# A fused SSM and two-MLP kernel on one Trainium2 core: token sums and rounding remainders of the next block pair moved to other places in the order, more tiles of their own for pair 1, and another order at the end

## The chip, the cores and the metric

One NeuronCore of a Trainium2 chip runs the whole program. The metric is the device time of one execution in microseconds (us). Five engines matter: TensorE (PE, matmuls into PSUM), VectorE (DVE), ScalarE (ACT), GpSimd (POOL) and SyncE (SP, which issues most transfers). Each runs its own list of instructions in order.

## The reference

The inputs are a small state-space layer and two MLPs on its output, all in float32. The second MLP is the part that the change touches.

```python
attn_out = _attn_ref(**attn_kwargs)            # 3072 tokens, 256 features
x = np.ascontiguousarray(attn_out.transpose(0, 2, 1, 3)).reshape(B * S, H * D)
h = x @ w_in                                   # 256 -> 2048
g = np.where(h > 0.0, h, np.exp(np.minimum(h, 0.0)) - 1.0)
x = g @ w_out                                  # 2048 -> 256
g = x @ w_gate                                 # 256 -> 1536
silu = g * (1.0 / (1.0 + np.exp(-g)))
val = x @ w_val                                # 256 -> 1536
out = silu * val @ w_out                       # 1536 -> 256, the second MLP's own w_out
```

(`w_gate`, `w_val` and the last `w_out` belong to the second MLP.)

## The kernel before, in words

Features lie on the 128 partitions and tokens along the free axis. The 3072 tokens are six blocks of 512. The state-space layer and the first MLP run block by block (16 steps of 128 hidden features each, 96 steps in all); the second MLP then takes the blocks in three pairs, p = 0, 1, 2, with 12 steps of 128 hidden features for a pair, 36 steps j = 0 to 35 (`s_step`, L729). The whole order is written out by hand: inside a step it is the order of the calls, and further work is hung on a step by `at(...)`. For the first MLP the table `late` holds work that follows a step; for the second MLP the table `hooks` holds it at four places of a step, `a` (before L770), `b` (before L777), `c` (before L784) and `d` (at the end), and `o` before the output products.

**Two parts for each operand.** A float32 value is split into a rounded part `h` (an ACT copy to the type float32r) and the remainder `l` = value minus `h` (a subtraction). A product then takes three matmuls, `h` x `h`, `l` x `h` and `h` x `l`. `x_hi` (L691) and `x_lo` (L706) do this for the tokens, `w2_hi` (L662) and `w2_lo` (L668) for the weights, `g_split` (L747) for the gated hidden values.

**Seven products for two blocks.** The gate and value products of a pair of blocks are formed with seven 128x512 products in place of eight. This needs sums of token tiles, `t3` = b22 - b12, `t1` = b12 - b11, `t2` = b22 - t1, `t4` = b21 - t2 (`x_sum`, L684; the b are quarters of the pair's tokens), and sums of weight tiles (`w2_sums`, L653, on POOL). The seven token operands of a step are, in order of use, b11, t2, t3, t1, b21, t4, b22.

**A step.** PE issues 33 matmuls: three each for b11 into PSUM tile `pa`, t2 into `pb`, t3 into `pd`, t1 into `pc`, then b21 onto `pa`, t4 onto `pd`, b22 onto `pc`, then twelve output products of the step before (`s_o`, L713, with the tiles `gh` and `gl`). The second product may be added onto `pd` only after DVE has read the first one. Beside it run, for each step:

```python
ACT  s1 = pa (L758);  s5 = pc (L764);  m0 = silu(pa) (L775);  m1 = silu(u2) (L781);  gh (L749), twice
DVE  u2 = s1 + pb (L762);  u3 = u2 + pd (L763);  u3 += s5 (L770);  s1 = u2 + pd (L777)
DVE  u2 = u2 + pc (L778);  m0 *= s1 (L779);  m1 *= u3 (L784)
POOL gl = m - gh (L750), twice
```

In steps 1 to 9 DVE has besides the remainder of a weight tile in two pieces (L670, at `b` and at `d`), ACT the rounding of it (L666), and POOL the four weight sums (L655 to L658), whose tile a transfer brings in (L651).

**The next pair.** For p = 1, 2 with e = 12p the sums of the pair's tokens stand on POOL at `c` of steps e-5 to e-2. The rounding (ACT, L704) and the remainders (DVE, t4's on POOL, L708) stand in steps e-3 to e-1; the remainders at `d`, b22's at `a` of step e. Operands b11, t2 and t3 of pair 1 have tiles of their own (b11 and t2 in the two staging tiles `v2` of the weights once these are done, t3 in a tile of the pool `w2h`); all others of pair 1 and all of pair 2 reuse pair 0's tiles.

**The end of a pair.** `s_end` (L720) copies the four PSUM outputs of a pair to SBUF, two on DVE (L724) and two on ACT (L726), and SP sends each to HBM (L727): for pairs 0 and 1 in the second step of the next pair, for pair 2 after the last step. Half of the copies go to two tiles `yo`, the other half into a finished token block.

## Time and profile before

| | us |
|---|---|
| median of three runs | 621.52 |
| the three runs | 621.55, 617.13, 621.52 |
| the profiled execution | 621.05 |
| its span, first to last instruction | 619.3 |
| mean granted clock of TensorE, share of full | 0.999 |

The profiled execution's time contains its span and what lies around it (1.75 us). The rows below are from this one execution. The times are from the start of the span; "idle before" is idle time of the engine directly before the instruction, with what ended it. A matmul's row lasts 0.39 us, but matmuls overlap: they begin 0.23 us apart, so the distance of starts tells PE's pace. The second MLP runs from 329.4 us to the end.

### The profile page before, as it was taken

To read this page: it belongs to the slowest core of one execution; us is meant where nothing else is said; L and a number is where in the kernel's file an instruction comes from. 1 tells how busy PE (TensorE), PEld (TensorE's weight loads), DVE (VectorE), ACT (ScalarE), POOL (GpSimd) and SP (SyncE) were. 2 spreads that over 40 slices of the span, in tenths; PEclk is the share of its full clock that TensorE was granted. 3 is DMA by queue.
4 is the path that set the end of the run, shared out by engine and by line. 5 is a ranking of instruction groups with operands and counts; after the bars stand their busy time and mean duration, and the time that the engine had idled before them with its cause. 6 is when DMAs were issued, how large, how long until landed. Compare 5 with 4: busy or idle time off the path is not lost.

```text
span 619.3 us, 9832 instructions
## 1 busy us (share of the span) xinstructions
PE 596.2 (96%) x3524; PEld 469.7 (76%) x3524; DVE 468.5 (76%) x676; ACT 369.6 (60%) x659; POOL 365.0 (59%) x326
## 2 busy tenths in 40 slices
PE   6899999999999999999999999978999998999997
PEld 4556667888888888778878777866888886888885
DVE  6898866768878789795644999899666679766664
ACT  1456657776668667776876555545544455544443
POOL 4444559997887887774765666756333456333332
PEclk9999999999999999999999999999999999999999
DMA  7698533345466666622010011100100000100001
GB/s 210 214 287 244 180 100 113 111 138 174 164 178 207 203 200 205 212 78 78 25 52 23 29 52 52 52 1 0 69 1 1 1 0 1 69 1 1 1 0 68
DMA packets 22744, 58.70 MB, mean 95 GB/s; under 512 B 3736, under 2 KB 6168, under 8 KB 22696
## 3 DMA queue, kind: packets, MB, share of 16 engines
q1 hardware_dynamic: 20664, 53.18, 27.6%
q10 hardware_dynamic: 2032, 4.90, 2.1%
q8 instruction: 27, 0.44, 0.3%
q14 instruction: 21, 0.17, 0.1%
HBM read 50.12 MB, written 7.96 MB: 94 GB/s over the span
## 4 chain that ended last, share of the span: by engine, by line
PE 62%; issue 10%; DVE 6%; POOL 5%; DMA 4%; ACT 1%; POOLq 0%; DVEq 0%; ACTq 0%
PE h L556 16%; PE c L605 15%; PE o L556 10%; PE pd L742 5%; POOL gl L750 5%; PE pa L742 5%; PE pc L742 4%; DMA w2e<-in_w 4%; PE pb L742 3%; PE cb L432 1%; PE y L509 1%; PE c L597 1%; DVE w2l L670 1%; DVE ident L763 1%; DVE ident L762 1%
## 5 line engine op out<-in xcount | busy, mean ns | idle before, releaser
L750 POOL TENSOR_TENSOR gl<-m,gh 128x512 fp32r<-128x512 f32 x71 | 94.6, 1333 | 133.6 <-ACT gh L749 133.6
L562 POOL TENSOR_TENSOR gl<-m,gh 128x512 fp32r<-128x512 f32 x80 | 110.6, 1383 | 43.5 <-ACT gh L561 42.1
L584 DVE SCALAR_TENSOR_TENSOR m<-m,h 128x512 f32<-128x512 f32 x96 | 65.5, 683 | 55.1 <-ACT m L583 53.2
L578 ACT ACTIVATE m<-h 128x512 f32<-128x512 f32 x96 | 56.8, 592 | 48.4 <-PE h L556 42.4
L556 PE MATMUL h<-xh,wih 128*128 128x512 f32 x192 | 81.3, 424 | 2.9 <-DVE x L477 1.9
L556 PE MATMUL h<-xh,wil 128*128 128x512 f32 x192 | 76.1, 396 | 0.0
L605 PE MATMUL c<-gh,woh 128*128 128x512 f32 x160 | 62.4, 390 | 0.0
L605 PE MATMUL c<-gh,wol 128*128 128x512 f32 x160 | 62.3, 389 | 0.0
L583 ACT ACTIVATE m<-m 128x512 f32<-128x512 f32 x96 | 59.8, 623 | 0.5
L556 PE MATMUL h<-xl,wih 128*128 128x512 f32 x192 | 59.8, 393 | 0.0
L781 ACT ACTIVATE m<-ident 128x512 f32<-128x512 f32 x36 | 22.8, 633 | 61.4 <-DVE ident L778 61.4
L556 PE MATMUL o<-gl,w2h 128*128 128x512 f32 x144 | 56.2, 390 | 0.4 <-POOL gl L750 0.4
L556 PE MATMUL o<-gh,w2h 128*128 128x512 f32 x144 | 56.2, 390 | 0.0
L556 PE MATMUL o<-gh,w2l 128*128 128x512 f32 x144 | 56.1, 390 | 0.0
L762 DVE TENSOR_TENSOR ident<-s,pb 128x512 f32<-128x512 f32 x36 | 24.6, 683 | 40.4 <-PE pb L742 36.6
L561 ACT ACTIVATE gh<-m 128x512 fp32r<-128x512 f32 x80 | 50.1, 626 | 6.0 <-DVE m L584 5.8
L605 PE MATMUL c<-gl,woh 128*128 128x512 f32 x160 | 50.9, 389 | 0.0
L556 PEld LDWEIGHTS h<-xh,wih 128*128 128x128 f32 x192 | 36.6, 190 | 15.4 <-DVE m L584 3.5
L393 POOL TENSOR_TENSOR xb<-xb,P 128x128 f32<-128x128 f32 x16 | 38.0, 2374 | 14.2 <-DVE P L387 14.2
L749 ACT ACTIVATE gh<-m 128x512 fp32r<-128x512 f32 x72 | 45.2, 628 | 1.2 <-DVE m L779 1.0
L764 ACT ACTIVATE x<-pc 128x512 f32<-128x512 f32 x36 | 21.5, 598 | 35.3 <-PE pc L742 35.3
L556 PEld LDWEIGHTS h<-xl,wih 128*128 128x128 f32 x192 | 36.5, 190 | 8.0
(226 smaller groups left out, 1470.9 us busy)
## 6 DMA issues: line engine op xcount, KB each, us to landing
w2e<-in_w SPq DMA_DIRECT2D x12, 768.0 KB
abc<-ac SPq DMA_DIRECT2D x16, 512.0 KB
bcraw<-in_bcs SPq DMA_DIRECT2D x32, 256.0 KB
w2e<-in_w SPq DMA_DIRECT2D x14, 512.0 KB
xb<-in_xbc SPq DMA_DIRECT2D x18, 256.0 KB
v2d<-w2e ACTq DMA_DIRECT2D x12, 384.0 KB
v<-v2d SPq DMA_DIRECT2D x12, 384.0 KB
out_y<-yo SPq DMA_DIRECT2D x6, 256.0 KB
```

Of the source, the lines that this page charges most:

```text
L393: nc.gpsimd.tensor_tensor(u["ct"], u["ct"], u["P"], ALU.mult)
L556: nc.tensor.matmul(dst, lhsT=l, rhs=r, start=first and i == 0, stop=last and i == len(ops) - 1, **kw)
L561: nc.scalar.activation(hi, src, AF.Copy)
L562: lo_eng.tensor_tensor(lo, src, hi.bitcast(F32), ALU.subtract)
L578: nc.scalar.activation(m, h, AF.Relu, scale=-1.0)
L583: nc.scalar.activation(m, m, AF.Exp, scale=-1.0)
L584: nc.vector.scalar_tensor_tensor(m, m, -1.0, h, ALU.add, ALU.max)
L605: nc.tensor.matmul(cps[b][m], lhsT=w[:, m * 128:(m + 1) * 128], rhs=r, start=f == 0 and w is wh and r is gh, stop=f == NF1 - 1 and r is gl)
L742: nc.tensor.matmul(ps[k], lhsT=l, rhs=r, start=first and i == 0, stop=i == 2, skip_group_check=True)
L749: nc.scalar.activation(hi, m, AF.Copy)
L750: eng.tensor_tensor(lo, m, hi.bitcast(F32), ALU.subtract)
L762: nc.vector.tensor_tensor(u2, s1, ps["b"], ALU.add)
```

## The change

**Sums.** The four sums of pair 1 go from POOL (steps 7 to 10) to DVE, into the last block of the first MLP (`late`, its steps 8 to 11, counted from 0). The four sums of pair 2 go from POOL (steps 19 to 22) to DVE at `b` of steps 15 to 18.

**Rounding and remainders.** Pair 1: t3 at `d` of step 0, b11 and t2 at `b` of step 10, t1 at `a` of step 11, b21 at `b` of step 11. Pair 2: b11, t2, t3, t1 at `b` of steps 18, 19, 20, 21, b21 at `b` of step 23. For both pairs t4 and b22 are rounded at `b` of step e-1; the remainder of t4 stays on POOL at `d` of step e-1, that of b22 on DVE at `a` of step e.

**Tiles.** Operand t1 of pair 1 gets a tile of its own too (pool `w2h`). The two tiles `yo` go; all outputs are copied into finished token blocks.

**The end.** In step 35 the `gl` of the first half is formed on DVE, not POOL; the four products of `gh` with both halves' weights for the first two outputs stand ahead of the two products with that `gl`; the copies of the first two outputs follow after both are done; the copy of the last output is cut in two, 256 columns on DVE and 256 on ACT.

```diff
-            if p == 1 and k < 3:
+            if p == 1 and k < 4:
...
-        y = x2[b - 1][:, m] if i else ph2["w2h"].tile([128, 512], F32, tag="yo", name="yo", bufs=2)
+        y, o = x2[min(2 * p + 2, NB - 2) + i][:, m], ops_.pop((p, i, m))
+        if cut:
+            nc.vector.tensor_copy(y[:, :256], o[:, :256])
+            nc.scalar.activation(y[:, 256:], o[:, 256:], AF.Copy)
...
-        g_split(j, 0, m0, nc.gpsimd)
+        end = j == NB // 2 * NF2 - 1
+        g_split(j, 0, m0, None if end else nc.gpsimd)
...
+        if end:
+            nc.vector.tensor_tensor(gt[j, 0][1], m0, gt[j, 0][0].bitcast(F32), ALU.subtract)
             g_split(j, 1, V.pop(j), nc.vector)
-            for i in range(2):
+            for k in range(2):
                 for m in range(2):
-                    s_o(j, i, m)
-                    s_end(p, i, m)
+                    s_o(j, 0, m, (slice(0, 2), slice(2, 3))[k])
+            for m in range(2):
+                s_end(p, 0, m)
+            for m in range(2):
+                s_o(j, 1, m)
+                s_end(p, 1, m, m)
...
-        for p in range(1, NB // 2):
+        for k, nm in enumerate(("t3", "t1", "t2", "t4")):
+            at(late, last_a + 9 + k, x_sum, 1, nm, nc.vector)
+            at(hooks, (NF2 + 3 + k, "b"), x_sum, 2, nm, nc.vector)
+        for p, where in ((1, dict(t3=(0, "d"), t1=(11, "a"), b11=(10, "b"), t2=(10, "b"))), (2, dict(b11=(18, "b"), t2=(19, "b"), t3=(20, "b"), t1=(21, "b")))):
             e = p * NF2
-            for k, nm in enumerate(("t3", "t1", "t2", "t4")):
-                at(hooks, (e - 5 + k, "c"), x_sum, p, nm, nc.gpsimd)
-            for k, nm in enumerate(OPS):
-                i, h, l = [(e - 3, "b", "d"), (e - 2, "b", "d"), (e - 2, "c", "d"), (e - 1, "b", "d"), (e - 1, "b", "d"), (e - 1, "c", "d"), (e - 1, "c", "a")][k]
-                at(hooks, (i, h), x_hi, p, nm)
-                at(hooks, (i + (l == "a"), l), x_lo, p, nm, nc.gpsimd if nm == "t4" else nc.vector)
+            for nm, z in where.items():
+                at(hooks, z, x_hi, p, nm)
+                at(hooks, z, x_lo, p, nm, nc.vector)
+            at(hooks, (e - 1, "b"), x_hi, p, "b21")
+            at(hooks, (e - 1, "b"), x_lo, p, "b21", nc.vector)
...
+            at(hooks, (e - 1, "d"), x_lo, p, "t4", nc.gpsimd)
+            at(hooks, (e, "a"), x_lo, p, "b22", nc.vector)
```

DVE's list before, from the end of step 9 (L670) through step 10 to the first instruction of step 11 (L762). `x_b11o`, `x_t2o` and `x_t3o` are tiles of pair 1, `x_67` the token blocks, `ident_65` holds u2 and u3:

```order
L670 TENSOR_TENSOR w2l_4366<-v_11_4268,w2h_4365 128x512
L708 TENSOR_TENSOR x_b11o<-x_67,x_b11o 128x512
L762 TENSOR_TENSOR ident_65<-s_4425,pb 128x512
L763 TENSOR_TENSOR ident_65<-ident_65,pd 128x512
L770 TENSOR_TENSOR ident_65<-ident_65,x_67 128x512
L777 TENSOR_TENSOR s_4425<-ident_65,pd 128x512
L778 TENSOR_TENSOR ident_65<-ident_65,pc 128x512
L779 TENSOR_TENSOR m_4444<-m_4444,s_4425 128x512
L784 TENSOR_TENSOR m_4451<-m_4451,ident_65 128x512
L708 TENSOR_TENSOR x_t2o<-x_67,x_t2o 128x512
L708 TENSOR_TENSOR x_t3o<-x_67,x_t3o 128x512
L762 TENSOR_TENSOR ident_65<-s_4491,pb 128x512
```

The changed kernel from the first instruction of step 10, behind the same L670, where L767, L768, L775, L782, L783, L784 and L790 are what L762, L763, L770, L777, L778, L779 and L784 were, up to the remainder of t1 in step 11:

```order
L767 TENSOR_TENSOR ident_65<-s_4426,pb 128x512
L768 TENSOR_TENSOR ident_65<-ident_65,pd 128x512
L775 TENSOR_TENSOR ident_65<-ident_65,x_67 128x512
L708 TENSOR_TENSOR x_b11o<-x_67,x_b11o 128x512
L708 TENSOR_TENSOR x_t2o<-x_67,x_t2o 128x512
L782 TENSOR_TENSOR s_4426<-ident_65,pd 128x512
L783 TENSOR_TENSOR ident_65<-ident_65,pc 128x512
L784 TENSOR_TENSOR m_4445<-m_4445,s_4426 128x512
L790 TENSOR_TENSOR m_4456<-m_4456,ident_65 128x512
L767 TENSOR_TENSOR ident_65<-s_4491,pb 128x512
L768 TENSOR_TENSOR ident_65<-ident_65,pd 128x512
L708 TENSOR_TENSOR x_t1o<-x_67,x_t1o 128x512
```

The remainders of b11 and t2 moved from the end of a step, ahead of L762, to the middle of step 10; that of t3 is no longer here, and that of t1 came ahead of step 11's L775.

POOL's list before, steps 9 to 11 (`gl` twice for a step, a sum L689 between them, t4's remainder at the end of step 11):

```order
L750 TENSOR_TENSOR gl<-m_4378,gh 128x512
L689 TENSOR_TENSOR x_67<-x_67 128x512
L750 TENSOR_TENSOR gl<-m_4387,gh 128x512
L750 TENSOR_TENSOR gl<-m_4444,gh 128x512
L689 TENSOR_TENSOR x_67<-x_67 128x512
L750 TENSOR_TENSOR gl<-m_4451,gh 128x512
L750 TENSOR_TENSOR gl<-m_4510,gh 128x512
L708 TENSOR_TENSOR x_t4l<-x_67,x_t4h 128x512
L750 TENSOR_TENSOR gl<-m_4517,gh 128x512
```

POOL's list in the changed kernel, the same steps:

```order
L756 TENSOR_TENSOR gl<-m_4383,gh 128x512
L756 TENSOR_TENSOR gl<-m_4390,gh 128x512
L756 TENSOR_TENSOR gl<-m_4445,gh 128x512
L756 TENSOR_TENSOR gl<-m_4456,gh 128x512
L756 TENSOR_TENSOR gl<-m_4513,gh 128x512
L708 TENSOR_TENSOR x_t4l<-x_67,x_t4h 128x512
L756 TENSOR_TENSOR gl<-m_4522,gh 128x512
```

The sums are gone from POOL, and t4's remainder keeps its place between the two `gl`.

PE's last matmuls before (`o_5398` to `o_5410` are the four outputs of pair 2):

```order
L556 MATMUL o_5398<-gh,w2h_4365 128x512
L556 MATMUL o_5398<-gh,w2l_4366 128x512
L556 MATMUL o_5398<-gl,w2h_4365 128x512
L556 MATMUL o_5402<-gh,w2h_4365 128x512
L556 MATMUL o_5402<-gh,w2l_4366 128x512
L556 MATMUL o_5402<-gl,w2h_4365 128x512
L556 MATMUL o_5406<-gh,w2h_4365 128x512
L556 MATMUL o_5406<-gh,w2l_4366 128x512
L556 MATMUL o_5406<-gl,w2h_4365 128x512
L556 MATMUL o_5410<-gh,w2h_4365 128x512
L556 MATMUL o_5410<-gh,w2l_4366 128x512
L556 MATMUL o_5410<-gl,w2h_4365 128x512
```

PE's last matmuls in the changed kernel (`o_5395` to `o_5407` are the same four):

```order
L720 MATMUL o_5395<-gh,w2h_4370 128x512
L720 MATMUL o_5395<-gh,w2l_4371 128x512
L720 MATMUL o_5399<-gh,w2h_4370 128x512
L720 MATMUL o_5399<-gh,w2l_4371 128x512
L720 MATMUL o_5395<-gl,w2h_4370 128x512
L720 MATMUL o_5399<-gl,w2h_4370 128x512
L720 MATMUL o_5403<-gh,w2h_4370 128x512
L720 MATMUL o_5403<-gh,w2l_4371 128x512
L720 MATMUL o_5403<-gl,w2h_4370 128x512
L720 MATMUL o_5407<-gh,w2h_4370 128x512
L720 MATMUL o_5407<-gh,w2l_4371 128x512
L720 MATMUL o_5407<-gl,w2h_4370 128x512
```

The two products with the first `gl` moved behind four products with `gh`.

## Rows read from the trace of the kernel before

**Rows 1.** The page, part 1: busy us (share of the span) and instructions of each engine.
```profile
PE 596.2 (96%) x3524; PEld 469.7 (76%) x3524; DVE 468.5 (76%) x676; ACT 369.6 (60%) x659; POOL 365.0 (59%) x326
```

**Rows 2.** Waits of PE in 329:620 us: waited for, us in total, times, longest us.
```profile
PE pd L742 <- DVE ident L763: 7.8, 8, 2.2
```

**Rows 3.** Timeline, PE: start us, us, engine line op out<-in xcount [idle before <-releaser].
```profile
345.74 0.39 PE L742 MATMUL pa<-x_b11h,w2h 128*128 128x512 f32 x1
...
400.42 0.39 PE L742 MATMUL pa<-x_b11h,w2h 128*128 128x512 f32 x1
...
409.34 0.39 PE L742 MATMUL pa<-x_b11h,w2h 128*128 128x512 f32 x1
...
415.06 0.50 PE L742 MATMUL pd<-x_t4h,w2h 128*128 128x512 f32 x1 [2.16 <-DVE ident L763]
...
444.65 0.39 PE L742 MATMUL pa<-x_b11o,w2h 128*128 128x512 f32 x1
...
511.97 0.39 PE L742 MATMUL pa<-x_b11o,w2h 128*128 128x512 f32 x1
...
529.70 0.39 PE L742 MATMUL pa<-x_b11h,w2h 128*128 128x512 f32 x1
...
604.50 0.39 PE L742 MATMUL pa<-x_b11h,w2h 128*128 128x512 f32 x1
```

**Rows 4.** Timeline, DVE: the end of step 9, step 12, the end of step 21.
```profile
410.11 1.82 DVE L670 TENSOR_TENSOR w2l<-v,w2h 128x512 fp32r<-128x512 f32 x1
...
411.85 1.77 DVE L708 TENSOR_TENSOR x_b11o<-x,x_b11o 128x512 fp32r<-128x512 f32 x1
...
414.32 0.69 DVE L763 TENSOR_TENSOR ident<-ident,pd 128x512 f32<-128x512 f32 x1
...
432.58 0.69 DVE L708 TENSOR_TENSOR x_b22l<-x,x_b22h 128x512 fp32r<-128x512 f32 x1
...
504.13 1.82 DVE L708 TENSOR_TENSOR x_b11l<-x,x_b11h 128x512 fp32r<-128x512 f32 x1
```

**Rows 5.** Timeline, POOL: the end of step 9 and the start of step 10.
```profile
410.09 1.29 POOL L750 TENSOR_TENSOR gl<-m,gh 128x512 fp32r<-128x512 f32 x1 [4.02 <-ACT gh L749]
...
411.34 1.74 POOL L689 TENSOR_TENSOR x<-x 128x512 f32<-128x512 f32 x1
...
413.04 1.72 POOL L750 TENSOR_TENSOR gl<-m,gh 128x512 fp32r<-128x512 f32 x1
```

**Rows 6.** Timeline, DVE and ACT: step 35, which begins at 604.50 us.
```profile
606.12 0.69 DVE L762 TENSOR_TENSOR ident<-s,pb 128x512 f32<-128x512 f32 x1 [1.88 <-PE pb L742]
...
607.48 0.60 ACT L764 ACTIVATE x<-pc 128x512 f32<-128x512 f32 x1 [0.98 <-PE pc L742]
...
608.16 0.60 ACT L775 ACTIVATE m<-pa 128x512 f32<-128x512 f32 x1
...
608.78 0.69 DVE L777 TENSOR_TENSOR s<-ident,pd 128x512 f32<-128x512 f32 x1
...
611.02 0.69 DVE L784 TENSOR_TENSOR m<-m,ident 128x512 f32<-128x512 f32 x1 [0.15 <-ACT m L781]
```

**Rows 7.** Timeline, ACT and DVE: from step 0 to step 1.
```profile
337.78 1.28 ACT L611 ACTIVATE x<-c 128x512 f32<-128x512 f32 x2 [0.79 <-PE c L605]
...
339.88 0.69 DVE L762 TENSOR_TENSOR ident<-s,pb 128x512 f32<-128x512 f32 x1 [2.68 <-ACT s L758]
...
340.67 0.69 DVE L763 TENSOR_TENSOR ident<-ident,pd 128x512 f32<-128x512 f32 x1
```

**Rows 8.** Timeline, POOL, PE and ACT: the end of the program.
```profile
611.61 1.29 POOL L750 TENSOR_TENSOR gl<-m,gh 128x512 fp32r<-128x512 f32 x1 [3.74 <-ACT gh L749]
...
612.95 0.50 PE L556 MATMUL o<-gl,w2h 128*128 128x512 f32 x1 [0.35 <-POOL gl L750]
...
615.54 0.60 ACT L726 ACTIVATE x<-o 128x512 f32<-128x512 f32 x1 [0.77 <-PE o L556]
```

**Rows 9.** Timeline, DVE: one step of the first MLP's last block.
```profile
316.46 0.69 DVE L584 SCALAR_TENSOR_TENSOR m<-m,h 128x512 f32<-128x512 f32 x1 [1.79 <-ACT m L583]
```

More of the change, by code (lines that the diff above doesn't have):

```diff
@@ L711, in s_half, with s_o, s_end @@
         return (ident8.rearrange("p h q -> p (h q)"))[:, 512 * i:512 * i + 512]
-    def s_o(j, i, m):
+    def s_o(j, i, m, part=slice(0, 3)):
         p, f = divmod(j, NF2)
-        if f == 0:
+        if (p, i, m) not in ops_:
             ops_[p, i, m] = ph2["ps"].tile([128, 512], F32, tag="h" if i else f"c{m}", name=f"o{i}{m}", bufs=2 if i else None)
         ms = slice(384 + m * 128, 384 + m * 128 + 128)
-        mm3(ops_[p, i, m], [([w[:, ms] for w in W2[f]], gt[j, i])], f == 0, f == NF2 - 1)
-    def s_end(p, i, m):
+        (wh, wl), (gh, gl) = [w[:, ms] for w in W2[f]], gt[j, i]
+        for k, (l, r) in list(enumerate(((wh, gh), (wl, gh), (wh, gl))))[part]:
+            nc.tensor.matmul(ops_[p, i, m], lhsT=l, rhs=r, start=f == 0 and k == 0, stop=f == NF2 - 1 and k == 2)
+    def s_end(p, i, m, cut=False):
         b = 2 * p + i
-        y = x2[b - 1][:, m] if i else ph2["w2h"].tile([128, 512], F32, tag="yo", name="yo", bufs=2)
-        if m == 0:
-            nc.vector.tensor_copy(y, ops_.pop((p, i, m)))
+        y, o = x2[min(2 * p + 2, NB - 2) + i][:, m], ops_.pop((p, i, m))
+        if cut:
+            nc.vector.tensor_copy(y[:, :256], o[:, :256])
+            nc.scalar.activation(y[:, 256:], o[:, 256:], AF.Copy)
+        elif m == 0:
+            nc.vector.tensor_copy(y, o)
         else:
-            nc.scalar.activation(y, ops_.pop((p, i, m)), AF.Copy)
+            nc.scalar.activation(y, o, AF.Copy)
         nc.sync.dma_start(out[m * 128:(m + 1) * 128, starts[b]:starts[b] + 512], y)
@@ L747, in g_split @@
         def g_split(j, i, m, eng):
-            hi, lo = [work.tile([128, 512], F32R, tag=f"g{z}", name=f"g{z}", bufs=LAG + 1) for z in "hl"]
+            hi, lo = gt[j, i] = [work.tile([128, 512], F32R, tag=f"g{z}", name=f"g{z}", bufs=LAG + 1) for z in "hl"]
             nc.scalar.activation(hi, m, AF.Copy)
-            eng.tensor_tensor(lo, m, hi.bitcast(F32), ALU.subtract)
-            gt[j, i] = hi, lo
+            if eng is not None:
+                eng.tensor_tensor(lo, m, hi.bitcast(F32), ALU.subtract)
         prod("a", 0, "b11", True)
```

3 lines of the change are left out of this document (2 added, 1 removed).

## The prediction

> **What bounds the kernel now.** I read the busy shares first: TensorE (PE) works 96% of the span, VectorE (DVE) 76%, ScalarE (ACT) 60%, GpSimd (POOL) 59% [rows 1]. With PE at 96% an edit off PE is worth only the PE idle time that it ends, so the second view is PE's waits inside the second MLP, from 329 us on. It names nearly one thing: PE stood 7.8 us in eight waits before the first matmul of `t4` into `pd`, released by DVE's L763 [rows 2]; besides, it waited 0.35 us for a `gl` of POOL at the very end [rows 8]. L763 adds the first half of `pd` to `u3`; until it has read `pd`, the second half can't be accumulated onto it.
>
> The timeline of PE shows what the waits cost. I number the 36 steps from 0 and take the first matmul into `pa` as a step's start. Steps 25 to 34 take (604.50 - 529.70) / 10 = 7.48 us each [rows 3]; that is 33 matmuls, 0.2267 us apart. Against that pace:
> - steps 2 to 8: 400.42 - 345.74 = 54.68 us for seven, 2.32 too many, 0.33 a step;
> - steps 9 to 13: 444.65 - 400.42 = 44.23 us for five, 6.83 too many;
> - steps 14 to 22: 511.97 - 444.65 = 67.32 us for nine, nothing;
> - steps 23 and 24: 529.70 - 511.97 = 17.73 us for two, 2.77 too many.
> The loss is larger than the idle time, since the first matmuls after a wait run late too: 9.60 us in the two places where the next pair of blocks is prepared, against 7.2 of idle time there.
>
> Why L763 is late is seen on DVE [rows 4]. At the end of step 9 two rounding remainders run one after the other, L670 of the weights (1.82 us) and L708 of `b11` (1.77), and only then L762 and L763; L763 ends at 415.01 and PE starts at 415.06 [rows 3, 4]. The same L708 takes 0.69 us at 432.58. The difference is POOL [rows 5]: its `gl` runs from 410.09 to 411.38, and the L670 that DVE began at 410.11 ends at 411.93, 0.55 later; POOL's sum L689 ends at 413.08, and DVE's L708 at 413.62, 0.54 later; that L689 itself took 1.74 instead of 1.29. DVE with two operands in SBUF and POOL exclude each other for a whole instruction, while L763, which reads one operand from PSUM, keeps its 0.69 us. So a remainder at the end of a step costs 1.8 us, because the `gl` of the same step starts there, and in mid-step about 0.7.
>
> The Trainium skill says the same in "SBUF — State Buffer", section "SBUF: two separate sides": the port pair shared by VectorE and GpSimd is an exclusive lock held for the whole instruction, by a VectorE operation with two SBUF inputs too, and the one that starts first wins. The trace agrees (0.54 us behind POOL's end, twice). It speaks against one part of the change: eight sums move from POOL to DVE, where each can also hold up a `gl`. By the rule that is at most 8 x 0.45 us on POOL, and since PE's only wait for POOL is the 0.35 us at the end, the sum below is the same by the one and the other.
>
> **The change part by part.**
> *Steps 9 to 12.* The remainders of pair 1 leave the ends of steps 9, 10 and 11 (five L708 on DVE). `b11` and `t2` now stand in mid-step 10, `t1` and `b21` in mid-step 11, `t3` at the end of step 0. Mid-step on DVE is the place before L777. In an undisturbed step (35, start 604.50) ACT's L764 ends 3.58 us after the start, its L775 runs 3.66 to 4.26, DVE's L777 starts at 4.28 and L784 ends at 7.21; the next L762 is due 1.62 into the next step, at 9.10 [rows 6].
> Step 10: the two ACT copies follow L775, 0.52 us apart, and end near 4.8 and 5.3; the remainders run 4.8 to 6.1, and L777 starts near 6.05, 1.75 late. Step 11: `t1` is copied after L764 to 4.1, its remainder ends at 4.85, L770 follows, the copy of `b21` ends near 5.1, its remainder near 6.05, and L777 starts 1.7 late. Queued behind are L778, L779 and L784, which then ends at 8.9 to 9.0, still before 9.10. `pd` is needed again at 7.48 + 6 x 0.227 = 8.84 and is free at 6.75; `pc` at 9.52, free at 7.5. So PE waits for none of it. Of the excess I leave steps 9 and 10 the 0.33 each that steps 2 to 8 pay (the weights' remainder still ends step 9), with 0 and 1.44 (step 9 now, which has a sum of POOL in it) as bounds for each. Step 13 is left nothing: step 25 has the same output copies and loses none [rows 3].
> *Steps 12 and 24, new edge.* The remainder of `t4` stays on POOL behind the last `gl` of its step; PE reads it 17 matmuls into the next step, at 11.33 after the start of step 11. The `gl` starts 7.11 after the start in step 35 [rows 6, 8], so 8.8 with the 1.7 from above; with 1.29 each it ends at 10.1, `t4` at 11.4. That is the edge: 0 to 0.8, I take 0.2. `b22` on DVE lies between two POOL instructions; due at 12.0, it can end at 12.4 if it meets the next `gl`: inside the same 0 to 0.8. In step 23 only `b21` is inserted, so `t4` has some 0.5 in hand; I take 0.1.
> Sum for steps 9 to 13: -6.83 + 0.66 + 0.20 = -5.97. For 23 and 24: -2.77 + 0.10 = -2.67. The sums and remainders of pair 2 in steps 15 to 21 add one or two instructions of 0.7 in mid-step, where the working for step 10 shows room for two. These sums overwrite tiles from which the output of pair 0 is sent, but those transfers are issued in step 13, 15 us earlier.
> *Step 0 to 1.* ACT's two L611 end at 339.06, and `t3`'s copy then delays L758 and DVE's L762 from 339.88 to about 340.25, so L763 ends at 341.75 instead of 341.36 [rows 7]; PE needs it at 338.26 + 15 x 0.2267 = 341.66. Cost 0.2, between 0 and 0.5.
> *First MLP.* Four sums on DVE where it idles, as the 1.79 us before one L584 [rows 9]; at 0.69 to 1.82 each they fit: 0. If one misses its gap, 0.4. POOL's loss of four sums in steps 7 to 10 may give steps 7 and 8 a little: 0, at best -0.4.
> *The end.* The last `gl` of half 0 moves from POOL (611.61 to 612.90) to DVE: 0.69 from 611.63, and four products of the rounded part stand ahead of its first use. PE was due at 604.50 + 35 x 0.2267 = 612.43 and started at 612.95 [rows 8]; that 0.52 goes, and the 0.1 of restart. The last copy (ACT, 0.60) is halved between DVE and ACT: 0.2 less at best. The four output transfers then come closer together and may queue, so -0.65, between -0.35 and -0.9.
> **Sum:** -5.97 - 2.67 + 0.20 - 0.65 = -9.09. The profiled execution took 621.05 us (span 619.3 and 1.75 around it), which gives 612.0. The median of the three runs, 621.52, is 0.5 above the profiled one; one of the three was 617.13.
>
> **The rivals.**
> 1. *The waits come back smaller.* Steps 9 and 10 lose the port to POOL as step 9 does now (409.34 - 400.42 - 7.48 = 1.44 each [rows 3]), and `b22` and `t4` hold PE in steps 12 and 24 (0.75 each): 4.4 us in place of my 0.96, so the gain is 9.1 - 3.4 = 5.7 and the time 615.4. For it: the margins of step 12 are tenths. Against: POOL's sums, which made step 9 late, are gone, and the 1.82 us remainder that ends step 21 at 504.13 costs step 22 nothing [rows 3, 4].
> 2. *Slower: DVE blocked in mid-step.* A remainder waits for its copy on ACT, and L777 stands behind it in DVE's queue. If L777 came more than 4.8 us (21 matmuls) after the last `t4` product, PE would wait for `pd` in each of the ten steps 10, 11, 15 to 21 and 23, at 1.35 apiece (the price of steps 23 and 24 now: 2.77 / 2): 621.05 - 9.6 - 0.65 + 13.5 = 624.3. Against: by rows 6 L777 comes at most 2 us late, and POOL has no sums left in these steps.
> 3. *It doesn't do what it says:* the new tiles share buffers with the weights' staging, so the copies could wait and the stalls only move. Then the end alone is gained: 620.4. Against: the last staging tile is read at the end of step 9, before the copies of step 10.
>
> **How the numbers follow.** Forecast 0.72, rival 1 0.18, rival 2 0.06, rival 3 0.04. Predicted: 612.0 us. Best bounds everywhere: -6.83 - 2.77 - 0.4 - 0.9 = -10.9, 610.15; a median from the lower of the run levels shown could be 3.9 below that, and I go down to 607. Upward, rival 1 plus the 0.5 between profile and median gives 615.9; I end at 616.5. A change over 1% is about what a measurement of this kernel can tell, here below 615.3: nearly all of the forecast and a quarter of rival 1 make 0.75 for faster; the rest of rival 1, the forecast's edge and rival 3 make 0.19; rival 2 leaves 0.06.
>
> **What would show it.** In the changed kernel's profile: PE's waits for L763 near 0.5 to 1.5 us in all; steps 10, 11, 23 at 7.48; every L708 on DVE but `t3` and `b22` near 0.69; the 0.35 us wait for the last `gl` gone. I am wrong if steps 10 to 12 or 24 are still over 8 us long, if PE waits for `t4` or `b22` remainders by more than 0.8, or if steps 15 to 21 leave the 7.48 pace.

## The result, and the profile after

The changed kernel takes 611.38 us (median of four runs, 611.34 to 611.60); the kernel before, run beside it, 621.29 (four runs, 617.13 to 621.55). The ratio is 0.9857, with a 95% interval of 0.9815 to 0.9898. The forecast was 612.0 us, with a range of 607.0 to 616.5. The profiled execution of the changed kernel took 611.60 us with a span of 609.8, 9.5 less than the span before (619.3).

Lines have moved: what was L742 (the products of a step) is L747, L556's output products are L720, L750 is L756, L758 is L763, L762 and L763 are L767 and L768, L764 is L769, L770 is L775, L777 is L782, L779 is L784, L784 is L790; the two halves of the cut copy are L726 and L727. I number the steps as in the prediction and call "loss" what a step takes beyond 7.48 us. DVE and POOL share a port to SBUF; an instruction "loses the port" when it has to wait until one of the other engine is done.

The busy shares and the chain that ended last, from the page of the changed kernel; the first row answers to [rows 1]:

```profile
PE 593.8 (97%) x3524; PEld 469.2 (77%) x3524; DVE 460.8 (76%) x686; ACT 368.9 (61%) x659; POOL 352.3 (58%) x317
...
PE 82%; DVE 3%; DMA 2%; ACT 1%; issue 1%; POOL 0%; ACTq 0%; DVEq 0%
```

PE's busy time is the same work in a shorter span, and 82% of the last chain is now PE itself (62% before). The waits of PE in the second MLP (329 us on) answer to [rows 2]. The matmuls have no row there any more; the weight loads, which run ahead of them, have two (us in total, times, longest). The first row here is that of the weight loads before, the other two are the changed kernel's:

```profile
PEld pd L742 <- DVE ident L763: 12.8, 13, 2.6
...
PEld pd L747 <- DVE ident L768: 3.4, 9, 0.5
PEld pd L747 <- POOL x_t4l L708: 0.2, 1, 0.2
```

The 7.8 us of idle matmuls before the first product of `t4` are gone (0.3 us in each of two repetitions). Of the 12.8 us of the weight loads 3.4 are left, in nine waits of at most 0.5 us (3.7 and 4.1 in the repetitions). The step starts on PE's timeline, which answer to [rows 3] (steps 0, 9, 10, 11, 14, 23, 25 and 35):

```profile
329.76 0.39 PE L747 MATMUL pa<-x_b11h,w2h 128*128 128x512 f32 x1
...
400.00 0.39 PE L747 MATMUL pa<-x_b11h,w2h 128*128 128x512 f32 x1
...
407.89 0.39 PE L747 MATMUL pa<-x_b11h,w2h 128*128 128x512 f32 x1
...
415.37 0.39 PE L747 MATMUL pa<-x_b11h,w2h 128*128 128x512 f32 x1
...
438.23 0.39 PE L747 MATMUL pa<-x_b11o,w2h 128*128 128x512 f32 x1
...
505.55 0.39 PE L747 MATMUL pa<-x_b11o,w2h 128*128 128x512 f32 x1
...
520.51 0.39 PE L747 MATMUL pa<-x_b11h,w2h 128*128 128x512 f32 x1
...
595.31 0.39 PE L747 MATMUL pa<-x_b11h,w2h 128*128 128x512 f32 x1
```

Step 10 is 415.37 - 407.89 = 7.48 us long, step 9 7.89 (8.92 before). From such starts the ledger of the span, against the same stretches before:

| stretch | loss before | loss after | gained | forecast |
|---|---|---|---|---|
| up to step 0 (start 329.42, now 329.76) | | | -0.34 | 0 |
| step 1 | 0 | 0.24 | -0.24 | -0.20 |
| steps 2 to 8 | 2.32 | 1.32 | 1.00 | 0 |
| steps 9 to 13 | 6.83 | 0.83 | 6.00 | 5.97 |
| steps 14 to 22, 25 to 34 | 0 | 0 | 0 | 0 |
| steps 23 and 24 | 2.77 | 0 | 2.77 | 2.67 |
| from the start of step 35 to the end | 14.80 | 14.49 | 0.31 | 0.65 |
| sum | | | 9.50 | 9.09 |

The two large terms came out to a tenth. The page prints a span to a tenth of a us; with the unrounded spans of the two traces, 619.275 and 609.812, the last stretch gains 0.27 and the sum is 9.46.

Of the 0.83 in steps 9 to 13, 0.41 is lost in step 9, 0 in step 10, 0.08 in step 11, 0.10 in step 12 and 0.24 in step 13. Step 13 lost the same 0.24 before. There an instruction of DVE in step 12 starts 0.47 us after the one ahead of it, where 0.1 is usual, and all behind it is some 0.36 late:

```profile
430.00 0.69 DVE L783 TENSOR_TENSOR ident<-ident,pc 128x512 f32<-128x512 f32 x1 [0.47 <-DVE s L782]
```

Such a hold of 0.35 to 0.36 us, for which the profile names no other engine, stands in every profile that loses time in step 13 (before the change it is L762 that starts 1.97 us after the start of step 13, not 1.62). Each time a transfer of instructions (queue q14 of the page) starts 0.65 to 0.68 us after the held instruction does. That the two belong together is seen in all these profiles; that fetching instructions causes the hold is not shown.

What stands in mid-step 10 now, and the edge of step 12, on the timeline of DVE and POOL with the matmul that reads `x_t4l` (they answer to [rows 4, 5]):

```profile
412.70 0.69 DVE L708 TENSOR_TENSOR x_b11o<-x,x_b11o 128x512 fp32r<-128x512 f32 x1 [0.51 <-ACT x_b11o L704]
413.31 0.69 DVE L708 TENSOR_TENSOR x_t2o<-x,x_t2o 128x512 fp32r<-128x512 f32 x1
413.91 0.68 DVE L782 TENSOR_TENSOR s<-ident,pd 128x512 f32<-128x512 f32 x1
...
425.39 1.29 POOL L708 TENSOR_TENSOR x_t4l<-x,x_t4h 128x512 fp32r<-128x512 f32 x1
425.97 1.26 DVE L708 TENSOR_TENSOR x_b22l<-x,x_b22h 128x512 fp32r<-128x512 f32 x1
...
426.78 0.45 PE L747 MATMUL pd<-x_t4l,w2h 128*128 128x512 f32 x1
```

The remainder of `b11` takes 0.69 us where it took 1.77 [rows 4], since no POOL instruction runs in mid-step, and L782 starts 413.91 - 407.89 = 6.02 us after the step's start (6.05 in the working). In step 12 `x_t4l` ends at 426.68, 0.02 before PE is due (the start of step 11, 415.37, plus 11.33): the edge was where the working put it. `x_b22l` began while POOL held the port, and ended 0.55 us after POOL's instruction did; the `gl` behind it on POOL then took 1.75 us.

The end, on the timeline (it answers to [rows 8]; the SP row is four transfers, of which the first is issued at its start):

```profile
604.12 0.69 DVE L729 COPY x<-o 128x512 f32<-128x512 f32 x1 [0.21 <-PE o L720]
...
604.84 2.07 SPq L732 DMA_DIRECT2D out_y<-x  x4
...
605.28 0.39 PE L720 MATMUL o<-gl,w2h 128*128 128x512 f32 x1
...
605.71 0.42 DVE L726 COPY x<-o 128x256 f32<-128x256 f32 x1
606.17 0.39 ACT L727 ACTIVATE x<-o 128x256 f32<-128x256 f32 x1 [1.22 <-DVE x L726]
```

PE's last matmul starts 9.97 us after the step's start where it was 10.62 (615.12 - 604.50): the 0.65 came. But ACT's half waits for DVE's half, so the last copy ends at 11.25 where it was 11.64, and the span ends only 0.31 sooner (0.27 by the unrounded spans).

### The profile page after: what moved, and what is told of

It reads as the page before. It is cut to its first block, busy times and chain, and to the rows that moved or that the text cites. A ratio compares the mean times of both kernels' runs of the same rounds, so it can differ in the third digit from the quotient of the medians.

```text
span 609.8 us, 9832 instructions
## 1 busy us (share of the span) xinstructions
PE 593.8 (97%) x3524; PEld 469.2 (77%) x3524; DVE 460.8 (76%) x686; ACT 368.9 (61%) x659; POOL 352.3 (58%) x317
## 4 chain that ended last, share of the span: by engine, by line
PE 82%; DVE 3%; DMA 2%; ACT 1%; issue 1%; POOL 0%; ACTq 0%; DVEq 0%
PE h L556 17%; PE o L720 16%; PE c L605 16%; PE pd L747 8%; PE pc L747 8%; PE pa L747 8%; PE pb L747 4%; DMA w2e<-in_w 2%; PE cb L432 1%; PE y L509 1%; PE c L597 1%; PE y L505 1%; ACT m L578 0%; ACT m L583 0%; DVE m L584 0%
## 5 line engine op out<-in xcount | busy, mean ns | idle before, releaser
L756 POOL TENSOR_TENSOR gl<-m,gh 128x512 fp32r<-128x512 f32 x70 | 92.7, 1327 | 134.4 <-ACT gh L754 117.4
L556 PE MATMUL h<-xh,wih 128*128 128x512 f32 x192 | 81.1, 422 | 2.5 <-DVE x L477 1.5
L556 PE MATMUL h<-xh,wil 128*128 128x512 f32 x192 | 75.9, 395 | 0.0
L556 PE MATMUL h<-xl,wih 128*128 128x512 f32 x192 | 59.7, 392 | 0.0
L720 PE MATMUL o<-gh,w2h 128*128 128x512 f32 x144 | 56.1, 389 | 0.0
L720 PE MATMUL o<-gh,w2l 128*128 128x512 f32 x144 | 56.0, 389 | 0.0
L720 PE MATMUL o<-gl,w2h 128*128 128x512 f32 x144 | 55.9, 389 | 0.0
L767 DVE TENSOR_TENSOR ident<-s,pb 128x512 f32<-128x512 f32 x36 | 24.7, 685 | 35.1 <-PE pb L747 31.9
L556 PEld LDWEIGHTS h<-xh,wih 128*128 128x128 f32 x192 | 36.5, 190 | 15.1 <-DVE m L584 3.7
L393 POOL TENSOR_TENSOR xb<-xb,P 128x128 f32<-128x128 f32 x16 | 38.0, 2374 | 14.2 <-DVE P L387 14.2
L556 PEld LDWEIGHTS h<-xh,wil 128*128 128x128 f32 x192 | 36.6, 191 | 7.6 <-issue 1.2
L556 PEld LDWEIGHTS h<-xl,wih 128*128 128x128 f32 x192 | 36.3, 189 | 8.0
```

Of the source, the lines that this page charges most:

```text
L393: nc.gpsimd.tensor_tensor(u["ct"], u["ct"], u["P"], ALU.mult)
L556: nc.tensor.matmul(dst, lhsT=l, rhs=r, start=first and i == 0, stop=last and i == len(ops) - 1, **kw)
L720: nc.tensor.matmul(ops_[p, i, m], lhsT=l, rhs=r, start=f == 0 and k == 0, stop=f == NF2 - 1 and k == 2)
L756: eng.tensor_tensor(lo, m, hi.bitcast(F32), ALU.subtract)
```

## The experiments

The length of the second MLP (from step 0's first matmul to the span's end) is given for each, since the first MLP ahead of it moves by some tenths from run to run (step 0 began between 328.4 and 330.6 us in all profiles but one). Before it is 289.88 us, after 280.04.

**1. Sums only.** The kernel before, with the eight sums on DVE at the changed times, and nothing else.

```diff
-                at(hooks, (e - 5 + k, "c"), x_sum, p, nm, nc.gpsimd)
+                at(*((late, last_a + 9 + k) if p == 1 else (hooks, (NF2 + 3 + k, "b"))), x_sum, p, nm, nc.vector)
```

> The kernel before with the eight sums alone moved to DVE; rounding, remainders, tiles and the end as before. Theory (port and place): of the two remainders at the end of a step the first still meets the gl, the second no longer meets a sum of POOL and takes 0.69 us, not 1.78. L763 comes 1.1 us earlier in steps 10, 11 and 23: their excess over 7.48 us falls from 2.48, 1.35, 1.40 to about 1.4, 0.3, 0.3; steps 12 and 24 keep 1.3, since t4's remainder on POOL still follows the gl. Steps 9 to 13 and 23, 24 lose about 5 us in place of 9.6; span near 614.7. Rival (the sums on POOL are all of it): 1 us or less is left, span near 611. Rival (the place at the end of a step is all of it): 9.6 us stay, span near 619.

Measured: 615.25 us (one run; before beside it 620.92), second MLP 283.83. Steps 9 to 13 lose 2.54 and steps 23 and 24 1.55, 4.09 in place of the 5 expected: the theory of port and place holds against both rivals, but step 10 lost 0.61 where it had 1.4. The end of step 11 in this kernel, DVE and POOL:

```profile
423.37 1.30 POOL L750 TENSOR_TENSOR gl<-m,gh 128x512 fp32r<-128x512 f32 x1 [3.97 <-ACT gh L749]
423.39 1.83 DVE L708 TENSOR_TENSOR x_t1l<-x,x_t1h 128x512 fp32r<-128x512 f32 x1
424.62 1.75 POOL L708 TENSOR_TENSOR x_t4l<-x,x_t4h 128x512 fp32r<-128x512 f32 x1
425.14 1.78 DVE L708 TENSOR_TENSOR x_b21l<-x,x_b21h 128x512 fp32r<-128x512 f32 x1
...
428.36 0.50 PE L742 MATMUL pd<-x_t4h,w2h 128*128 128x512 f32 x1 [0.89 <-DVE ident L763]
```

The two engines take turns: each DVE remainder ends 0.55 us after the POOL instruction that it met, and the POOL instruction that follows takes 1.75 in place of 1.29. Where only the `gl` is left beside two remainders (the ends of steps 9, 10 and 22), one of the two takes 0.68 or 0.69 (the second, but at step 22 the first) and the next step loses 0.61, 0.28 and 0.22; where `t4`'s remainder still stands behind the `gl` (these rows, and the end of step 23) the next step still loses 1.3.

**2. Places only,** twice: the changed kernel with the sums back on POOL (at their new times) and the old end (the lines that bring back the old end are not printed here).

```diff
-            at(late, last_a + 9 + k, x_sum, 1, nm, nc.vector)
-            at(hooks, (NF2 + 3 + k, "b"), x_sum, 2, nm, nc.vector)
+            at(late, last_a + 9 + k, x_sum, 1, nm, nc.gpsimd)
+            at(hooks, (NF2 + 3 + k, "b"), x_sum, 2, nm, nc.gpsimd)
...
```

> The changed places for rounding and remainders and the tile for t1, with the sums at their new times but on POOL, and the end as before. Theory (port and place): the sums meet nothing on DVE's late part of a step there; steps 9 to 13 lose 0.8 as in the changed kernel, 23 and 24 nothing; span 609.8 + 0.3 to 0.65 for the end = 610.1 to 610.5. Rival (sums on POOL cost by themselves): 1 us or more in each of the steps 15 to 18, span over 614.

> The kernel with the changed places and GpSimd's sums, once more, since its first run lost 3.5 us near 265 us of the span, in the first MLP, ahead of all that was edited. Theory (a weight load that landed late by chance): no wait of PE over 0.5 us and no fall of the granted clock at 262 to 270 us; about 612.3 us, second MLP 280.9 us. Rival (the edit brings it about): 616 us again, with the same wait of some 2.6 us at the same place.

Measured: 616.16 us the first time (one run), a miss, but with a second MLP of 280.94 and nothing lost in steps 14 to 34, so neither theory holds for it. The time was lost in the first MLP. PE's row there, and two windows of the core behind it (length, busy time and count of PE, PEld, DVE, ACT and POOL, granted clock, DMA share, GB/s):

```profile
265.52 0.50 PE L556 MATMUL h<-xh,wih 128*128 128x512 f32 x1 [2.63 <-DVE m L584]
```

```profile
266.00:268.00 2.00, 2.00 (x7) 1.57 (x6) 2.00 (x4) 1.42 (x3) 1.78 (x2) 0.52 0.00 0
268.00:270.00 2.00, 2.00 (x7) 1.33 (x5) 2.00 (x3) 1.09 (x2) 0.32 (x1) 0.63 0.76 246
```

A transfer of the first MLP's weights landed late (ACT idle 4.45 us for it at 262.25), PE stood 2.63 us, and then ran 2 us at half of its clock (1.2 in place of 2.4 GHz) and part of the next two. The second execution of the same program has no such wait and the clock at 1.00 in all these windows: 612.75 us in the profile, 611.30 in the other run, second MLP 280.60. So the edit alone doesn't bring it about. The old end takes 15.03 and 15.04 us in this kernel, not 14.80: here L768 of step 35 starts 0.35 us late, with the same kind of hold as in step 13 above. From step 0 to the start of step 35 it is 265.91 and 265.56 us, and 265.55 to 266.14 in three profiles of the changed kernel: which engine forms the sums is worth nothing once the remainders have moved.

**3. One remainder, and two, at the end of a step,** without sums on POOL. Pair 2's `b11`, `t2`, `t3`, `t1` singly at the end of steps 18 to 21, then two each at the end of steps 19 and 21. The rounding stays at `b` of the same step, in lines that are not printed here.

```diff
-(2, dict(b11=(18, "b"), t2=(19, "b"), t3=(20, "b"), t1=(21, "b")))
+(2, dict(b11=(18, "d"), t2=(19, "d"), t3=(20, "d"), t1=(21, "d")))
...
+(2, dict(b11=(19, "d"), t2=(19, "d"), t3=(21, "d"), t1=(21, "d")))
```

> The changed kernel with the remainders of b11, t2, t3, t1 of pair 2 at the end of steps 18 to 21, one in each, not in mid-step. Theory (port and place): each meets a gl and takes 1.82 us, L763 of the next step is done about 0.3 us before PE needs it, and no step from 14 to 25 leaves 7.48 us; span as in the changed kernel, 609.8. Rival (the place alone): 1.35 us for each of four steps, span near 615.

> The same with two remainders at the end of step 19 (b11, t2) and two at the end of step 21 (t3, t1), no sums on POOL beside them. Theory: the first takes 1.82 us, the second 0.69 from a free port, so L763 is 0.3 us too late in steps 20 and 22 and these lose 0.3 to 0.7 each; span 610.4 to 611.2. Rival (two remainders at the end of a step cost what they cost before, whatever POOL does): 1.35 to 1.4 each, span near 612.6.

Measured: singly 612.38 us (one run), second MLP 280.19, steps 14 to 34 lose nothing although three of the four remainders take 1.81 or 1.82 (the first, `b11`, began 0.02 us behind the `gl`, got the port and takes 0.69). Two at a time 613.43 us (one run), second MLP 281.06, steps 20 and 22 lose 0.24 each, a little under the 0.3 to 0.7 expected. DVE in the second kernel:

```profile
484.11 1.81 DVE L708 TENSOR_TENSOR x_b11l<-x,x_b11h 128x512 fp32r<-128x512 f32 x1
485.84 0.68 DVE L708 TENSOR_TENSOR x_t2l<-x,x_t2h 128x512 fp32r<-128x512 f32 x1
```

So the price is not "a remainder at a step's end": one that loses the port is covered where it starts early enough (0.35 us before step 20 begins, in both kernels), a second that finds it free costs 0.24 here (0.22 to 0.61 in experiment 1), a second that loses it too costs 1.3 (experiment 1). What the places cure are pairs that both meet POOL.

**4. The end only.** The kernel before with the changed end: the diff's parts in `s_o`, `s_end` and `s_step`, but the outputs still in the old tiles, and none of the moved places, sums and tiles.

> The kernel before with the changed end alone (the last gl of half 0 on VectorE, another order of the last products, the last copy cut). Theory (the end gains what the first output transfer gains, 0.2 to 0.3 us, and the rest of the 9.5 us lies in steps 0 to 24): the span ends 14.5 us after the start of step 35 instead of 14.8; steps 9 to 13 and 23, 24 lose 6.8 and 2.8 us as in the kernel before; about 620.7 us. What steps 2 to 8 lose is a second sample of the old order: between 1.3 and 2.4 us if it is chance. Rival (the end gains the forecast 0.65): 14.15.

Measured: 621.33 us (one run; before beside it 621.87), second MLP 289.26, the span ends 14.48 us after the start of step 35, as the theory has it. The other half of the expectation missed: steps 9 to 13 lost 8.06 and steps 23 and 24 only 1.30. Step 10 lost 3.97 in place of 2.48 (DVE, POOL and PE; here L770 is the addition that frees `pd`, L748 the products):

```profile
412.18 1.74 POOL L689 TENSOR_TENSOR x<-x 128x512 f32<-128x512 f32 x1
412.70 1.77 DVE L708 TENSOR_TENSOR x_b11o<-x,x_b11o 128x512 fp32r<-128x512 f32 x1
...
415.91 0.79 PE L748 MATMUL pd<-x_t4h,w2h 128*128 128x512 f32 x1 [2.14 <-DVE ident L770]
416.51 0.63 PE L748 MATMUL pd<-x_t4h,w2l 128*128 128x512 f32 x1
```

```profile
416.00:418.00 2.00, 2.00 (x5) 1.61 (x6) 1.06 (x2) 0.00 (x0) 0.00 (x0) 0.50 0.00 0
418.00:420.00 2.00, 2.00 (x7) 1.57 (x7) 1.41 (x3) 0.34 (x1) 0.00 (x0) 0.69 0.00 0
```

The wait is the one of the kernel before, remainder behind POOL's sum; but here the granted clock fell to 0.50 behind it, with matmuls 0.43 us apart. In the profile of the kernel before, the clock stayed at 1.00 behind a wait of 2.16 us, and step 10 lost 2.48. Why it fell here and not there is open. Steps 2 to 8 lost 2.26 (2.32 before).

Step 23 lost 0.26 in place of 1.40, and the port settles why. At the end of step 22 DVE's first remainder begins 0.02 us behind the `gl`, and yet gets the port; POOL's `gl` (here L757) waits:

```profile
513.64 1.85 POOL L757 TENSOR_TENSOR gl<-m,gh 128x512 fp32r<-128x512 f32 x1 [3.29 <-ACT gh L755]
513.66 0.68 DVE L708 TENSOR_TENSOR x_t2l<-x,x_t2h 128x512 fp32r<-128x512 f32 x1
```

Before, the same two began 0.03 us apart (511.64 and 511.67), and the remainder took 1.82. Around the starts of steps 0 to 25 in all fourteen profiles a remainder on DVE begins 0.02 us behind a POOL instruction 39 times; it got the port in 10 of them. At 0.03 to 0.06 us behind it lost all 65 times. So near-ties fall either way from run to run. This one is worth 1.1 us.

**5. The changed kernel again,** twice.

> The changed kernel once more, as the neighbour of the two kernels that follow. Theory: 611.4 us, the second MLP from step 0 to the span's end near 280.0 us as in the first profile; steps 9 to 13 lose under 1 us, steps 14 to 34 nothing; steps 1 to 8 lose something between 1.3 and 2.3 us, another amount than the 1.56 us of the first profile, if what they lose is chance. Rival (what steps 1 to 8 lose is set by the order of the instructions): the same 1.56 us within 0.1, step by step.

> The changed kernel a third time, as the neighbour of the two above on the same chip: 611.4 us, the end 14.5 us after the start of step 35, steps 1 to 8 losing 1.3 to 2.3 us and steps 9 to 13 under 1 us.

Measured: 611.48 us (four runs; ratio 0.9857, 0.9820 to 0.9895) and 611.64 (four; 0.9860, 0.9844 to 0.9877). Steps 9 to 13 lose 0.99 and 0.73, the end takes 14.52 and 14.54. Steps 1 to 8 lose 1.64 and 2.25, and by step it is another pattern than the first profile's 1.56: step 5 lost 0 there and 0.32 here, step 3 0.14, 0.05 and 0.58. How a step loses, in the first repetition (step 5):

```profile
369.10 0.39 PE L747 MATMUL pa<-x_b11h,w2h 128*128 128x512 f32 x1
369.39 1.30 POOL L756 TENSOR_TENSOR gl<-m,gh 128x512 fp32r<-128x512 f32 x1 [0.42 <-ACT gh L754]
369.44 1.79 DVE L670 TENSOR_TENSOR w2l<-v,w2h 128x512 fp32r<-128x512 f32 x1
```

The weights' remainder loses the port by some 0.05 us. In step 5 it starts 0.34 us after the step, and 0.32 is lost; in step 6, where it loses the port too, 0.08 after it, and 0.04 is lost. The same in steps 4 (0.39: 0.36), 7 (0.33: 0.33) and 9 (0.59: 0.58). A step that lost time brings the next remainder earlier, and in step 8 it came before the `gl`, took 0.95 and lost nothing. In step 6 of the first profile it began 0.58 us after the step and 0.02 behind the `gl`, got the port (0.68 us), and nothing was lost; in step 9 of the first repetition it began 0.59 after and 0.03 behind, lost the port, and 0.58 was lost. So much of the 1.00 gained in steps 2 to 8 is spread: these steps lose 1.32, 1.42 and 2.01 in three profiles of the changed kernel, and 1.32 to 2.01 in all eight that have the changed places and the weights' remainders untouched. Both profiles of the old order lie above all of these (2.26 and 2.32; 1.76 with the sums alone moved), so part of it may be the change's; two profiles don't settle it.

**6. The last copy whole.** The changed kernel with `s_end(p, 1, m)` in place of `s_end(p, 1, m, m)`.

> The changed kernel, with the last output copy whole on ScalarE (0.60 us) in place of two halves. Theory (the halves run one behind the other, 0.42 + 0.39 us and a gap, so the cut costs): last copy ends about 10.99 us after the start of step 35 instead of 11.25, the end is 0.25 us shorter, about 611.2 us beside 611.4. Rival (the cut pays, as halves that ran together would): the end is 0.2 us longer, 611.6. Steps 0 to 34 are as in the changed kernel by both.

Measured: 611.05 us (four runs, 610.11 to 613.98; before beside it 619.71, ratio 0.9861, 0.9821 to 0.9902), second MLP 279.67, not to be told from the changed kernel. The last copy does end 0.25 us sooner, at 11.00 after the step's start (step 35 starts at 593.81), but the span ends at 14.49 as with the cut. Both sides of the expectation fall. The copy in this kernel, and then the last 5 us of the DMA engines (603.30 to 608.30 in 40 slices: busy share in tenths, and what they moved):

```profile
604.21 0.60 ACT L731 ACTIVATE x<-o 128x512 f32<-128x512 f32 x1 [0.76 <-PE o L720]
```

```profile
DMA  0000000899999999999999999988100000000000
GB/s 0 0 0 0 0 0 0 344 393 410 442 360 443 361 442 377 442 344 442 393 426 442 344 459 360 459 344 328 33 0 0 0 0 0 0 0 0 0 0 0
```

The four outputs are 1.05 MB and leave as one stream of some 400 GB/s, 2.6 us without a hole, which starts about 0.85 us after the first issue. From the first issue to the end of the span it is 14.49 - 9.53 = 4.96 us here, 4.96, 4.99 and 5.00 in the three profiles of the changed kernel, 5.09 in the kernel before, whose stream has one hole (from unrounded spans 4.97 to 4.98 in these four, 5.07 before). A copy behind the first changes nothing as long as the stream is fed.

**7. The first copy cut,** on top of experiment 9: two halves of the first output with a transfer for each. The last copy is whole, and the second output is copied by DVE, not ACT (these lines are not printed here).

```diff
             nc.vector.tensor_copy(y[:, :256], o[:, :256])
+            nc.sync.dma_start(out[m * 128:(m + 1) * 128, starts[b]:starts[b] + 256], y[:, :256])
             nc.scalar.activation(y[:, 256:], o[:, 256:], AF.Copy)
+            nc.sync.dma_start(out[m * 128:(m + 1) * 128, starts[b] + 256:starts[b] + 512], y[:, 256:])
```

> The same, and at the end the first of the four output copies, not the last, is cut in two with a transfer for each half (VectorE 256 columns, transfer, ScalarE 256 columns, transfer). Theory (the end is set by the four transfers, which run without a gap at some 400 GB/s from the first issue on; the last copy has time in hand): the first issue comes 0.27 us earlier after the start of step 35 (9.26 instead of 9.53), and the span ends 14.2 to 14.35 us after that start instead of 14.5. Rival (the last copy or the last transfer's own latency sets the end): 14.5 or more, since the two extra copies and the fifth transfer only add. Whole kernel 609.3 us by the one, 609.6 by the other.

Measured: 611.90 us (five runs), second MLP 281.08, the first issue at 9.27 as expected, the end at 14.51: no gain, and the theory's 14.2 to 14.35 falls. The second half's copy on ACT again starts only behind DVE's, so its transfer is issued 0.42 us after the first (604.86 and 605.28), and the next one 0.47 later; a half of 128 KB lasts some 0.33 us at 400 GB/s. The stream has holes (busy shares of 0.2 and 0.3 between the first transfers), which take back what the early start gave.

**8. The weights' second remainder in mid-step,** and the last copy whole.

```diff
-            at(hooks, (f - 2, "d"), w2_lo, f, 1)
+            at(hooks, (f - 2, "b"), w2_lo, f, 1)
```

> The same as the kernel with the whole last copy, and besides the weights' second remainder (on VectorE, two SBUF operands, 1.8 us when it meets GpSimd) stands in mid-step, ahead of the sigmoid's products, and no longer at the end of steps 0 to 9. Theory (what steps 1 to 9 still lose is this remainder meeting GpSimd's gl at a step's end, ahead of the addition that frees pd): each of these steps loses at most 0.05 us, under 0.5 us in all instead of 1.3 to 2.3; second MLP 278.2 to 278.6 us, about 609.6 us. Rival (the loss comes from elsewhere, or the remainder makes the products late in mid-step): steps 1 to 9 lose 1.3 us or more, 611.2 us or longer.

Measured: 610.74 us (four runs; 0.9850, 0.9817 to 0.9882), second MLP 279.63; steps 1 to 9 lose 1.80. The theory falls: the loss came back by another way. Step 6 of this kernel, DVE and ACT:

```profile
376.80 0.39 PE L747 MATMUL pa<-x_b11h,w2h 128*128 128x512 f32 x1
376.87 0.68 DVE L784 TENSOR_TENSOR m<-m,s 128x512 f32<-128x512 f32 x1
377.59 0.64 ACT L754 ACTIVATE gh<-m 128x512 fp32r<-128x512 f32 x1
378.13 0.58 ACT L763 ACTIVATE s<-pa 128x512 f32<-128x512 f32 x1
...
378.74 0.69 DVE L767 TENSOR_TENSOR ident<-s,pb 128x512 f32<-128x512 f32 x1 [0.34 <-ACT s L763]
```

Two remainders in mid-step take 1.95 us beside POOL's weight sums, L784 slips 0.07 into the next step, `gh` behind it on ACT delays the copy L763 (1.33 after the step's start), and L767 starts at 1.94 where 1.62 is undisturbed: a loss of 0.20.

**9. The two remainders in two places,** the first behind L768, the second in mid-step, the rounding a step earlier; the last copy is whole.

```diff
-            at(hooks, (f - 2, "a"), w2_hi, f, 0)
+            at(hooks, (f - 3, "b") if f > NHL else (0, "d"), w2_hi, f, 0)
...
-            at(hooks, (f - 2, "b"), w2_hi, f, 1)
-            at(hooks, (f - 2, "b"), w2_lo, f, 0)
-            at(hooks, (f - 2, "d"), w2_lo, f, 1)
+            at(hooks, (f - 2, "a"), w2_hi, f, 1)
+            at(hooks, (f - 2, "a"), w2_lo, f, 0)
+            at(hooks, (f - 2, "b"), w2_lo, f, 1)
```

> The kernel with the whole last copy, and each half of a weight's remainder in a place of its own: the first behind VectorE's addition that frees pd (ahead of the addition of ScalarE's copy), the second in mid-step, none at a step's end; the copy that the first needs is made a step earlier. Theory (the loss of steps 1 to 9 is a port-taking instruction between the last product of VectorE and the addition that frees pd; the two remainders together in mid-step failed since the products then ended 0.1 us inside the next step and delayed ScalarE's copies): the sigmoid's products start at most 6.05 us after the start of a step, steps 2 to 9 lose under 0.3 us in all (step 1 keeps 0.22 for t3), second MLP 278.3 to 278.8 us beside 279.7 to 280.3, about 609.5 us. Rival (one port conflict is exchanged for another, VectorE is simply short of time in these steps): they lose 1.3 us or more again, 611 us.

Measured: 612.39 us (four runs; 0.9876, 0.9860 to 0.9891), second MLP 281.17, steps 1 to 9 lose 2.5: the rival holds. Of this 0.85 is step 1, where the first weight's rounding on ACT now stands ahead of `t3`'s; steps 2 to 9 lose 1.68. POOL's weight sums L655 to L658 alternate with the remainders (1.36 to 1.40, and 0.95 for each), and the products L782 start 6.27 us after the start of step 3. This kernel and that of experiment 7 also lose 0.77 and 0.75 in step 24, where their program is the changed kernel's:

```profile
517.26 1.29 POOL L756 TENSOR_TENSOR gl<-m,gh 128x512 fp32r<-128x512 f32 x1
517.37 1.73 DVE L708 TENSOR_TENSOR x_b22l<-x,x_b22h 128x512 fp32r<-128x512 f32 x1
...
519.15 0.50 PE L747 MATMUL pc<-x_b22l,w2h 128*128 128x512 f32 x1 [0.22 <-DVE x_b22l L708]
```

L767 began 1.97 us after the step's start there, not 1.62; so `x_b22l` came 0.11 us behind the `gl` in place of ahead of it, took 1.73 us instead of 0.84, and PE waited. L767 was late by the same kind of hold as DVE's in step 13 above, and a transfer of instructions again starts 0.65 us after it: step 13, where the changed kernel has the hold, loses nothing here. It shows that the edge at `b22` is real: 0 or 0.75, decided by a few tenths.

None of these versions beats the changed kernel by more than the intervals.

## Why the prediction was right

- **The two large terms** (5.97 and 2.67 forecast, 6.00 and 2.77 measured) rest on one reading of [rows 4, 5]: a remainder costs 0.7 or 1.8 us by whether POOL is at work. Every remainder of pairs 1 and 2 on DVE but `b22`'s took 0.68 or 0.69 us after, `t3`'s too. Experiments 1 to 3 show the reading by taking parts away: sums alone bring 6.05 us of the second MLP, places alone 8.9 and 9.3, both with the end 9.2 to 9.84. The parts overlap; in my sum I had not separated them, and nearly all of it is the places. The new tile for `t1` and the tiles `yo` were not varied by themselves; pair 2, which gets no new tile, loses nothing in steps 23 and 24 either.
- **Luck in the parts.** For steps 9 to 13 the working left 0.33, 0.33, 0, 0.20 and 0 (0.86 in all); measured were 0.41, 0, 0.08, 0.10 and 0.24 (0.83). Step 10 came out better since the weights' remainder ahead of it began within 0.03 us of its start in all three profiles, early enough to cost 0 to 0.03 whoever had the port. Step 13 was left nothing since step 25 loses none, which overlooked the 0.24 that it lost before. The two misses cancel: that the sum is right to 0.03 is luck, its size is not.
- **The Trainium skill**, "SBUF — State Buffer", section "SBUF: two separate sides", has the port shared by the two engines as an exclusive lock that the one who starts first wins. The trace agrees in both directions (`x_b22l` 0.84 or 1.26 us when it started in time to have the next `gl` wait, 1.73 when 0.11 behind it), except in the near-ties: of 39 remainders that began 0.02 us behind POOL, 10 got the port (experiment 4).
- **Step 0 to 1:** 0.20 forecast, 0.24 measured, 0.22 and 0.24 in the repetitions.
- **The new edge in steps 12 and 24:** 0.2 and 0.1 forecast; in three profiles step 11 loses 0.04 to 0.08, step 12 0.10 to 0.11, step 24 nothing. Experiments 7 and 9 found its upper end, 0.8, in step 24.
- **Rival 1** (waits come back smaller) had 1.44 each for steps 9 and 10: measured 0.41 and 0, 0.31 to 0.58 and 0.03 in the repetitions. **Rival 2** (DVE blocked in mid-step) needed L777, now L782, more than 4.8 us behind the last product of `t4`; it came only 1.74 later than undisturbed (6.02 after the step's start instead of 4.28), and steps 15 to 21 kept 7.48. (The price in its sum, 2.77 / 2, is 1.39, not 1.35, which makes 624.7 and changes nothing.) It has a milder form: in experiment 8 two slow remainders there made L782 2.05 us late in step 5, and step 6 lost 0.20. **Rival 3** falls with the rows of step 10: the copies don't wait.
- **Mis-sized: "The end"**, -0.65 forecast, -0.31 measured (0.26 to 0.27 by the unrounded spans of three profiles), outside its own -0.35 to -0.9. PE's part came in full (0.65 at the last matmul). The step that failed is "the last copy is halved between DVE and ACT: 0.2 less at best", with transfers that "may queue": the halves run one behind the other, 0.25 us more than the whole copy, and even that doesn't count, for the stream of four transfers sets the end (experiment 6). The gain is what the first issue gained, 9.71 to 9.53 after the step's start, and the hole in the old stream. The sum also overlooked that the four products of `gh` hold back the first output: its copy starts 8.81 us after the step's start, only 0.18 sooner than before (8.99). DVE's `gl` was done at 7.81, before PE's turn for it in the old order (35 x 0.2267 = 7.93); so by this estimate `gl` on DVE alone would have started that copy some 0.4 us sooner. It wasn't tried.
- **Not in the sum:** 1.00 us in steps 2 to 8 and -0.34 ahead of step 0. The -0.34 lies inside what the same program does from run to run (step 0 starts at 328.42 to 329.76 in three profiles); of the 1.00, some 0.7 does (1.32 to 2.01 in three profiles, experiment 5), and whether the rest is the change's is open. They hid the miss at the end: without them the ledger would be 8.84, a time of about 612.2.
